# The attention tails of a fused attention and expert kernel on one core: one block tile for the tail keys of v, one tile for the tails of k and q, and another figure in the planner

## The chip, the core and the metric

The kernel runs on one core of one Trainium2 chip. The core's engines each run their own list of instructions in order: TensorE (PE, with its weight loads shown apart as PEld), VectorE (DVE), ScalarE (ACT), GpSimd (POOL), and SyncE (SP), which here only issues DMA transfers. Semaphores tie the lists together. The metric is the time of one execution in microseconds, the median of several; less is better. Before the change it is 1306.65 us, the median of three runs from 1305.46 to 1310.91 us.

## What is computed

There are 8 batches of 8 heads, 576 rows in each and 64 columns in a head, all in fp32. The first half is an attention that keeps the 32 largest scores of each row; the second sends each of the 4608 rows to one of 8 experts.

```python
scores = scale * np.matmul(q, k.transpose(0, 1, 3, 2))
kth = np.partition(scores, -top_k, axis=-1)[..., -top_k:-top_k + 1]
scores = np.where(scores >= kth, scores, -1e9)
attn = np.exp(scores - max) / (sum + 1e-9)
x = np.matmul(attn, v)                     # heads side by side: [4608, 512]
e_idx = np.argmax(x @ w_gate + modality_bias[modality_id], axis=1)
out = gate_w * (np.maximum(x @ w1[e], 0.0) @ w2[e])      # e = e_idx of the row
```

## The kernel before

**Pairs and tiles.** Two heads make a pair; there are 32 pairs. The 576 rows of a head are 4 blocks of 128 and a tail of 64. A pair is 9 tiles of 128 query rows: tiles 0 to 7 are the four blocks of the two heads in turn, and tile 8 holds the tail rows of both heads together. So there are 288 tiles, and the main loop (L865) makes one step for each, with a pipeline behind it: in step i the scores of tile i+2 are multiplied (`qk`, L324), the largest 32 values of tile i are looked for on VectorE (`subs`, `chain`, `find`, `pick`, L337 to L388), the masked weights of tile i-7 are formed there too (`keep`, L399), and tile i-9 is transposed on TensorE (`trans`, L414). VectorE's and GpSimd's parts are interleaved by hand.

**Weights by v.** `av` (L424) multiplies the transposed weights by v in five chunks of keys: four of 128 keys and a last one, c = 4, with the 64 tail keys. It runs three times for a pair: at tile 3 (query blocks 0 and 1), at tile 7 (blocks 2 and 3), both with 256 columns, and at tile 8 (the query tails, 64 columns). Each chunk is one matmul for each head; the two heads write the two halves of the output's partitions. The transposed tails of the two heads lie in the two halves of the partitions of `PT[:, :, 4]`, so in chunk 4 the tail of head 1 is read from partitions 64 to 127, for which `load` puts the tail of v of head 1 there a second time (L132). `av` hands its chunks out in pieces (AV3, AV7), one for a step.

**Tails of k and q.** `load` brings them as two tiles `kt` and `qt` of 64 partitions each. `prep(p, "t")` transposes both (L273), in step 0 of the pair before; the result goes through `split` to the operands of `qk`.

**The planner.** Expert work starts as soon as enough rows of finished batches are sorted. A list `moe` holds its pieces in order: transposes of the gathered rows `xg` (L690), the first layer (L702: `w1b`, `xgT`), the second layer (L714: `w2b`, `hT`). The loop keeps a credit `spare_pe`. Each step adds STEP = 3.3 us and takes off what the step's own TensorE work costs by the table COST (L53): 0.49 for one chunk of `av` with 256 columns. While the credit is over zero, pieces of `moe` are issued and their costs (0.22, 0.44 a matmul, 0.88) taken off (L960 to L971). An expert's slot of 256 rows is 8 such transposes, 32 products of the first layer and 16 of the second as they are written. 12 slots are started inside the loop; what is left of the list is issued after it (L1144). Then come the remaining slots with weights split in two parts (L1111, L1127).

Of the kernel before, what the change touches and what calls it, by code (L numbers as in the profile page):

```python
# [9 lines left out]
FT = mybir.dt.float32  # L10
# [39 lines left out]
PB = 4  # L50
AV3 = (0, 3, 5)
AV7 = (0, 2, 5)
COST = {"trans": 0.5, "qk": 0.5, "mix": 1.12, "rest": 0.22, "t": 0.11, "prep": 0.43, "logits": 1.2, "xrow": 0.54, "av": 0.49, "av8": 0.17}  # L53
RN = 6
QO = 0
FAST = 1
# [13 lines left out]
def kernel(  # L70
# [13 lines left out]
    V, A, G, PE, SP = nc.vector, nc.scalar, nc.gpsimd, nc.tensor, nc.sync  # L84
    B, H, S, D = q.shape
# [11 lines left out]
    const = ctx.enter_context(tc.tile_pool(name="const", bufs=1))  # L97
# [7 lines left out]
    ld = att.enter_context(tc.tile_pool(name="ld", bufs=2))  # L105
# [4 lines left out]


    LD, PR, T = {}, {}, {}
    PAUSE = lambda: None

    def load(p, what, b=None):

        o = LD.setdefault(p, {})
        h0 = 2 * (p % HP)
        for nm in what:
            src = {"k": k, "q": q, "v": v}[nm]  # L120
            g = src[p // HP] if b is None else src[ds(b, 1)].rearrange("o h s d -> (o h) s d")
            t = ld.tile([128 if nm == "v" else 64, 2, D], FT, name=nm + "t", bufs=2 if nm == "v" else 1)
            m = ld.tile([128, 2, 4, D] if nm == "v" else [128, 4, 2, D], FT, name=nm + "m", bufs=2 if nm == "v" else 1)
            if nm == "v":
                SP.dma_start(m.rearrange("p h c d -> p h (c d)"),
                             g[h0:h0 + 2, 0:512, :].rearrange("h (p c) d -> p h (c d)", c=4))
            else:
                for h in range(2):
                    SP.dma_start(m[:, :, h, :], g[h0 + h, 0:512, :].rearrange("(p c) d -> p c d", c=4))
            SP.dma_start(t[:64], g[h0:h0 + 2, 512:, :].rearrange("h p d -> p h d"))  # L130
            if nm == "v":
                SP.dma_start(t[64:, 1, :], g[h0 + 1, 512:, :])  # L132
            o[nm] = (m, t)

    load(0, "kq")
# [4 lines left out]
    idf = const.tile([128, 128], FT, name="idf")  # L140
# [26 lines left out]
    Pb = [wk.tile([128, 2 * S], FT, name=f"P{i}", bufs=1) for i in range(2)]  # L167
    Pm = const.tile([128, 640], FT, name="Pm")
    G.memset(Pm[:, S:], 0.0)
    xT = const.tile([128, HP + 2, S], FT, name="xT")  # L170
    xTs = lambda b: [xT[:, (b * HP + hp) % (HP + 2)] for hp in range(HP)]
    PT = const.tile([128, 4, 9, 128], FT, name="PT")
# [91 lines left out]
    def prep(p, part):  # L264


        d = PR.setdefault(p, {})
        if "st" not in d:
            d["st"] = wk.tile([128, 2, 2, S], FR, name="st", bufs=1)
        if part == "t":  # L270
            ps = psX.tile([128, 2, 64], FT, name="X")
            for x, nm in enumerate("kq"):
                PE.matmul(ps[:, x], LD[p][nm][1], idf[:64, :64], start=(x == 0), stop=False, is_transpose=True,  # L273
                          skip_group_check=True)
            split(*(d["st"][:, x, :, 512:] for x in range(2)), ps)
            return
        st = d["st"][:, :, "kq".index(part)]
        ps = psX.tile([128, 512], FT, name="X")
        for c in range(4):
            PE.matmul(ps[:, c * 128:(c + 1) * 128], LD[p][part][0][:, c], idf, start=(c == 0), stop=False,  # L280
                      is_transpose=True, skip_group_check=True)
        split(*(st[:, x, :512] for x in range(2)), ps)

        half = lambda x: slice(x * 64, x * 64 + 64)
        if part == "k":
            d["ks"] = wk.tile([128, 2, 2, S], FR, name="ks", bufs=2)
        else:
            d["qs"] = wk.tile([128, 2, S], FR, name="qs", bufs=2)

        def stack(h, queues=(SP, SP)):  # L290
            for v in range(2):
                if part == "k":
                    for a, b, o in ((0, S, 0),) if h == 0 else ((0, 512, 64), (512, S, -512)):
                        queues[v].dma_start(d["ks"][half(v), :, h, a + o:b + o].bitcast(FT), st[half(h), :, a:b].bitcast(FT))
                else:
                    queues[v].dma_start(d["qs"][half(v), h, :].bitcast(FT), st[half(h), v, :].bitcast(FT))

        for h in range(2):
            late_pe.append(lambda h=h, **o: stack(h, **o))
# [124 lines left out]
    def av(p, j, x):  # L424

        vm, vt = LD[p]["v"]
        w = 256 if j < 8 else 64
        st = {}

        def part(c0, c1):  # L430
            if c0 == 0:
                st["po"] = psX.tile([128, 256], FT, name="X")
            po = st["po"]
            for c in range(c0, c1):
                for h in range(2):
                    K = slice(0, 128) if c < 4 else slice(64, 128) if h and j < 8 else slice(0, 64)
                    l = vm[:, h, c, :] if c < 4 else vt[K, h, :]
                    if j < 8:
                        r = PT[K, j // 2 - 1:j // 2 + 1, c + 5 * h if c < 4 else 4, :]
                    else:  # L440
                        r = PT[K, 1, 4 + c, h * 64:h * 64 + 64]
                    o = po[h * 64:h * 64 + 64, :w]
                    PE.matmul(o.rearrange("p (a b) -> p a b", a=2) if j < 8 else o, l, r, start=(c == 0), stop=(c == 4))  # L443
            if c1 == 5:
                o = (j // 4) * 256
                xev.append(lambda: A.activation(x[:, o:o + w], po[:, :w], AF.Copy))
        cut = {3: AV3, 7: AV7, 8: (0, 5)}[j]
        return [((b - a) * COST["av" if j < 8 else "av8"], lambda a=a, b=b: part(a, b)) for a, b in zip(cut, cut[1:])]

# [415 lines left out]
    for i in range(LAST):  # L865
# [4 lines left out]

        cost = COST["trans"] * ok(i - TL)
        p, j = divmod(i, 9)
# [6 lines left out]
        if ok(i + QL):  # L879
            cost += COST["mix" if (i + QL) % 9 == 8 else "qk"]  # L880
        if QO == 0:
# [23 lines left out]
        for f in lp:  # L905
            f()
        cost += COST["rest"] * (len(lp) > 0)
        if p + 1 < NPAIR and j in PREP:
            prep(p + 1, PREP[j])
            cost += COST["t" if PREP[j] == "t" else "prep"]  # L910
        if p + 2 < NPAIR and j in LJ:
# [3 lines left out]
        b1, r = divmod(i - (TL + 2), 36)  # L915
        b1 -= 1
        if 0 <= b1 < B:
# [3 lines left out]
            if r == rl[0]:  # L921
                rows_of[b1] = logits(b1, xTs(b1))
                cost += COST["logits"]
            if r == rl[1]:
# [12 lines left out]
            if b1 == 0 and r == 8:  # L937
                head, tail = first_slot()
# [10 lines left out]
        if avs:  # L949
            c, f = avs.popleft()  # L950
            f()
            cost += c
        if ok(u) and u % 9 in (3, 7, 8):
            f = av(u // 9, u % 9, xTs(u // 36)[(u // 9) % HP])
# [6 lines left out]
        while seen[0] and spare_pe > 0:  # L961
# [4 lines left out]
            c, f, new = moe[0]  # L966
# [23 lines left out]
        for x in range(RN if rush else 0):  # L990
            f = rush.popleft() if rush else PAUSE
# [6 lines left out]
        for x in range(SN - len(small_)):  # L998
            f = side.popleft() if side and not rush else PAUSE
# [192 lines left out]
    ld = att.enter_context(tc.tile_pool(name="ldb", bufs=2))  # L1192
# [96 lines left out]
```

## Time and profile before

| | |
|---|---|
| median of 3 runs | 1306.65 us |
| profiled execution | 1310.04 us, its span 1308.2 us |
| TensorE busy | 1220.9 us, 93% of the span |
| VectorE busy | 1163.1 us, 89% |
| ScalarE, GpSimd busy | 1016.5 us, 685.9 us |
| last main tile formed on VectorE (L399) | starts at 1071.16 us |
| first matmul of the slots after the loop (L1111) | starts at 1122.55 us |

Times in the profile count from the start of the span. A matmul of fp32 operands appears as two records in the trace: the 768 products of v's 128-key chunks are 1536 records. A record's duration holds the way through the array, so neighbours overlap, and what one costs TensorE is read from the distance of the starts. The granted clock of TensorE is shown as a share of 2.4 GHz.

### The profile page before, as it was taken

What the parts mean: (1) busy time and instruction counts of PE and PEld (TensorE: products, weight loads), DVE (VectorE), ACT (ScalarE), POOL (GpSimd) and SP (SyncE); (2) the same over time, 40 slices, a digit from 0 to 9 for tenths busy, and PEclk for the clock granted to TensorE, in tenths of its full rate; (3) what the DMA queues carried; (4) which work ended last, traced back from release to release, by engine and by line L of the source; (5) the groups of instructions that cost most, each with busy time, mean ns of one, the idle gap of its engine ahead of it and who ended that gap; (6) DMA issues with size and microseconds to landing.
All of it is one profiled execution on the core that took longest, in us unless ns stands there. A gap on an engine that the chain in (4) does not pass through costs nothing. (4 is left out here: it accounts for less than half of the span.)

```text
span 1308.2 us, 29253 instructions
## 1 busy us (share of the span) xinstructions
PE 1220.9 (93%) x8149; PEld 926.4 (71%) x8149; DVE 1163.1 (89%) x5918; ACT 1016.5 (78%) x2037; POOL 685.9 (52%) x1330
## 2 busy tenths in 40 slices
PE   5888888899998999999999999999999998999986
PEld 4666666676775867677676767777676756789885
DVE  3999999999999999999999999999999973667752
ACT  3899988889887888898889889998888863445542
POOL 2555557546675557655856585658556753110110
PEclk7899999999999999999999999999999999999998
DMA  5565334676447746576656556666664534657550
GB/s 117 136 187 129 84 83 115 168 198 154 123 120 192 184 130 168 155 177 158 190 148 158 156 153 181 143 159 186 152 154 121 164 104 141 233 176 262 207 169 15
DMA packets 206791, 201.08 MB, mean 154 GB/s; under 512 B 106222, under 2 KB 153326, under 8 KB 206609
## 3 DMA queue, kind: packets, MB, share of 16 engines
q1 hardware_dynamic: 200400, 179.48, 52.0%
q0 software_dynamic: 6208, 19.54, 4.1%
q8 instruction: 70, 1.15, 0.4%
q14 instruction: 113, 0.92, 0.2%
HBM read 118.63 MB, written 24.23 MB: 109 GB/s over the span
## 5 line engine op out<-in xcount | busy, mean ns | idle before, releaser
L337 DVE MAX8 cand<-Ssb 128x8 f32<-128x82 f32 (+1 forms) x2016 | 433.4, 231 | 19.7 <-ACT Ssb L330 19.6
L375 POOL TENSOR_TENSOR y<-Ssb,K 128x576 f32<-128x576 f32 x288 | 368.1, 1278 | 9.8 <-ACT K L369 9.7
L324 PE MATMUL S<-ks,qs 128*128 128x288 f32 x1024 | 234.7, 352 | 48.6 <-ACT Ssb L330 27.8
L330 ACT ACTIVATE Ssb<-S 128x576 f32<-128x576 f32 x288 | 188.6, 655 | 91.3 <-PE S L324 77.0
L369 ACT ACTIVATE K<-Ssb,n 128x576 bf16<-128x576 f32 x288 | 227.3, 789 | 18.0 <-POOL y L375 17.7
L324 PEld LDWEIGHTS S<-ks,qs 128*128 128x128 f32 x1024 | 159.5, 193 | 105.5 <-ACT Ssb L330 42.7
L393 ACT ACTIVATE ex<-Ssb,sm 128x576 f32<-128x576 f32 x288 | 225.6, 783 | 0.0
L399 DVE SCALAR_TENSOR_TENSOR P<-Ssb,kth,ex 128x576 f32<-128x576 f32 x256 | 214.4, 838 | 2.6 <-PE T L414 1.4
L379 DVE MAX8 mg<-y 128x8 f32<-128x576 f32 x288 | 214.8, 746 | 2.0 <-POOL y L375 2.0
L422 ACT ACTIVATE PT<-T 128x640 f32<-128x640 f32 (+1 forms) x288 | 190.8, 663 | 10.0 <-PE T L414 10.0
L702 PE MATMUL E<-xgT,w1b 128*128 128x256 f32 x768 | 188.8, 389 | 4.1 <-ACT hT L706 2.7
L714 PE MATMUL E<-w2b,hT 128*128 128x512 f32 x384 | 185.6, 605 | 1.7 <-ACT ot L724 1.0
L414 PE MATMUL T<-idf,P 128*128 128x128 f32 x1152 | 170.8, 276 | 0.0
L443 PE MATMUL X<-PT,vm 128*64 128x256 f32 (+1 forms) x1536 | 160.7, 338 | 4.3 <-ACT st L261 2.5
L702 PEld LDWEIGHTS E<-xgT,w1b 128*128 128x128 f32 x768 | 139.9, 192 | 34.7 <-issue 5.8
L403 POOL TENSOR_SCALAR spare<-P 1x1 f32<-1x1 f32 x256 | 48.2, 188 | 209.6 <-DVE mg L348 193.6
L414 PEld LDWEIGHTS T<-idf,P 128*128 128x128 f32 x1152 | 136.8, 142 | 5.3 <-issue 2.7
L362 POOL TENSOR_SCALAR n<-mg 128x1 f32<-128x1 f32 x288 | 66.7, 232 | 114.2 <-DVE mg L350 102.9
L443 PEld LDWEIGHTS X<-PT,vm 128*64 128x64 f32 x1536 | 79.8, 136 | 56.4 <-issue 26.8
L714 PEld LDWEIGHTS E<-w2b,hT 128*128 128x128 f32 x384 | 66.0, 190 | 62.8 <-issue 54.2
L1133 POOL DMA_INDIRECT out_dram<-ot,tk x14 | 14.1, 1005 | 129.9 <-ACT ot L1132 129.9
L480 POOL TENSOR_TENSOR x<-x,rd 128x256 f32<-128x256 f32 (+1 forms) x80 | 52.7, 663 | 39.2 <-ACT x L484 36.2
(209 smaller groups left out, 2309.6 us busy)
## 6 DMA issues: line engine op xcount, KB each, us to landing
w1b<-in_moe_w_dram SPq DMA_DIRECT2D x76, 512.0 KB
w2b<-in_moe_w_dram SPq DMA_DIRECT2D x76, 512.0 KB
ks<-st SPq DMA_DIRECT2D x64, 288.0 KB
qs<-st SPq DMA_DIRECT2D x128, 144.0 KB
ks<-st SPq DMA_DIRECT2D x62, 256.0 KB
xg<-xs SPq DMA_DIRECT2D x19, 516.0 KB
km<-in_k_dram SPq DMA_DIRECT2D x64, 128.0 KB
qm<-in_q_dram SPq DMA_DIRECT2D x64, 128.0 KB
```

The costliest lines, as they stand in the source:

```text
L324: PE.matmul(ps[:, hf, u - a:v - a], l, d["ks"][:, x, h, u + o:v + o], start=(n == 0), stop=(n == len(terms) - 1), skip_group_check=(j == 8))
L337: return [lambda s=s: V.max(c[:, s * 8:s * 8 + 8], T[i]["S"][:, bnd[s]:bnd[s + 1]]) for s in range(NSUB)]
L369: A.activation(t["K"], t["S"], AF.Sign, scale=2.0 ** -24 - 1.0, bias=t["n"][:, 1, i % 3:i % 3 + 1], accum_out=t["n"][:, 0, i % 3:i % 3 + 1])
L375: G.tensor_tensor(t["y"], t["S"], t["K"], op=OP.mult)
L379: V.max(t["mg"][:, i % 3, 24:32], t["y"])
L393: A.activation(t["ex"], t["S"], AF.Exp, bias=t["s"][:, i % 3:i % 3 + 1])
L399: V.scalar_tensor_tensor(t["P"], t["S"], kth[:, i:i + 1], t["ex"], op0=OP.is_ge, op1=OP.mult, accum_out=dn)
L414: PE.transpose(T[i]["pt"][:, x, :], (Pm if c == 4 else Pb[c % 2])[:, h * 512 + x * 128:h * 512 + x * 128 + 128], idf)
L422: A.activation(o, T[i]["pt"][:, :n], AF.Copy)
L443: PE.matmul(o.rearrange("p (a b) -> p a b", a=2) if j < 8 else o, l, r, start=(c == 0), stop=(c == 4))
L702: PE.matmul(ps[:, f % 2], w1b[:, c, f * 128:(f + 1) * 128], xgT[:, c, :], start=(c == 0), stop=(c == KC - 1))
L714: PE.matmul(o["py"], hT[:, f, t * 128:(t + 1) * 128], w2b[:, f, :], start=(f == 0), stop=(f == FC - 1))
```

## The change

Three edits. (1) The tail tile of v becomes a fixed tile `vtb[p % 2]` of 128 partitions and three slots of 64 columns, zeroed once by VectorE. Head 0's tail goes to partitions 0 to 63 of slot 0, head 1's to partitions 64 to 127 of slot 1 and to partitions 0 to 63 of slot 2. Slots 0 and 1 together are a block-diagonal 128 by 128 operand, so chunk 4 with 256 columns is one matmul for both heads. For the query tails (tile 8) chunk 4 stays one matmul a head, now with all 128 partitions, of which the upper half is zero. (2) The tails of k and q are the two partition halves of one tile `kqt` and take one transpose. (3) COST["av"] is 0.46 instead of 0.49. Lines after the first edits lie some 7 to 11 lower in the changed file: L273, L324, L414, L443, L690, L702, L714, L1082 and L1111 of before are L280, L331, L421, L443 and L453, L701, L713, L725, L1093 and L1122 there.

```diff
-COST = {..., "av": 0.49, "av8": 0.17}
+COST = {..., "av": 0.46, "av8": 0.17}
...
+    vtb = [const.tile([128, 3, 64], FT, name=f"vt{i}") for i in range(2)]
...
+            if nm == "k":
+                o["kq"] = ld.tile([128, 2, D], FT, name="kqt", bufs=1)
+            t = vtb[p % 2] if nm == "v" else o["kq"][:64] if nm == "k" else o["kq"][64:]
...
-            SP.dma_start(t[:64], g[h0:h0 + 2, 512:, :].rearrange("h p d -> p h d"))
             if nm == "v":
+                tail = g[h0:h0 + 2, 512:, :].rearrange("h p d -> p h d")
+                SP.dma_start(t[:64, 0:3:2, :], tail)
                 SP.dma_start(t[64:, 1, :], g[h0 + 1, 512:, :])
+            else:
+                SP.dma_start(t, g[h0:h0 + 2, 512:, :].rearrange("h p d -> p h d"))
...
+    for t in vtb:
+        V.memset(t, 0.0)
...
-            for x, nm in enumerate("kq"):
-                PE.matmul(ps[:, x], LD[p][nm][1], idf[:64, :64], start=(x == 0), ...)
+            PE.matmul(ps.rearrange("p a b -> p (a b)"), LD[p]["kq"], idf, start=True, ...)
...
+                if c == 4 and j < 8:
+                    PE.matmul(po[:, :w]..., vt[:, 0:2, :].rearrange("p h d -> p (h d)"),
+                              PT[:, j // 2 - 1:j // 2 + 1, 4, :], start=False, stop=True, ...)
+                    continue
                 for h in range(2):
-                    K = slice(0, 128) if c < 4 else slice(64, 128) if h and j < 8 else slice(0, 64)
-                    l = vm[:, h, c, :] if c < 4 else vt[K, h, :]
+                    l = vm[:, h, c, :] if c < 4 else vt[:, 2 * h, :]
```

The edits move instructions on TensorE. The first place is one step of pair 29, with the transposes of its tile 0 of the pair before in the pipeline, the tails `kt` and `qt` (now `kqt`), and the two last pieces of `av` of a pair. Before:

```order
L414 MATMUL T<-idf,P_122 128x128 x4
L273 MATMUL X<-idf,kt 128x64
L273 MATMUL X<-idf,qt 128x64
L443 MATMUL X<-PT,vm 64x256 x4
L443 MATMUL X<-PT,vt 64x256 x2
L443 MATMUL X<-PT,vm 64x64 x8
L443 MATMUL X<-PT,vt 64x64 x2
```

The same place in the changed kernel:

```order
L421 MATMUL T<-idf,P_123 128x128 x4
L280 MATMUL X<-idf,kqt 128x128
L453 MATMUL X<-PT,vm 64x256 x4
L443 MATMUL X<-PT,vt_81 128x256
L453 MATMUL X<-PT,vm 64x64 x8
L453 MATMUL X<-PT,vt_81 64x64 x2
```

Two tail transposes are one, and the two `vt` products with 256 columns are one. Over the 32 pairs that is 64 products and 32 transposes less as they are written; no other count on TensorE changes.

The second place is the end of the main loop on TensorE: from the transposes of tile 283 to those of tile 287 (`Pm`, the last). Before:

```order
L414 MATMUL T<-idf,P_122 128x128 x4
L443 MATMUL X<-PT,vm 64x256 x6
L714 MATMUL E<-w2b,hT 128x512 x2
L414 MATMUL T<-idf,P_122 128x128 x5
L443 MATMUL X<-PT,vm 64x256 x2
L443 MATMUL X<-PT,vt 64x256 x2
L714 MATMUL E<-w2b,hT 128x512 x2
L414 MATMUL T<-idf,P_123 128x128 x4
L714 MATMUL E<-w2b,hT 128x512
L414 MATMUL T<-idf,P_123 128x128 x5
L690 MATMUL E<-idf,xg 128x128 x2
L414 MATMUL T<-idf,Pm 128x128 x5
```

In the changed kernel:

```order
L421 MATMUL T<-idf,P_123 128x128 x4
L453 MATMUL X<-PT,vm 64x256 x6
L701 MATMUL E<-idf,xg 128x128 x4
L421 MATMUL T<-idf,P_123 128x128 x5
L453 MATMUL X<-PT,vm 64x256 x2
L443 MATMUL X<-PT,vt_82 128x256
L713 MATMUL E<-xgT,w1b 128x256 x6
L421 MATMUL T<-idf,P_124 128x128 x4
L713 MATMUL E<-xgT,w1b 128x256 x2
L421 MATMUL T<-idf,P_124 128x128 x5
L713 MATMUL E<-xgT,w1b 128x256 x2
L421 MATMUL T<-idf,Pm 128x128 x5
```

The last of the twelve slots began with two of its `xg` transposes just ahead of tile 287; it now begins at tile 282 and has done 10 of its 32 first-layer products by tile 287.

The third place is after the loop on TensorE, from the last of the products that rank the rows of batch 7 (`ohb`) to the first product of the slots after the loop. Before:

```order
L535 MATMUL X<-ohb_148,onesb 128x8
L702 MATMUL E<-xgT,w1b 128x256 x16
L714 MATMUL E<-w2b,hT 128x512 x10
L1082 MATMUL X<-idf,xg 128x128 x8
L714 MATMUL E<-w2b,hT 128x512 x6
L1111 MATMUL X<-xgh,w1h 128x256
```

In the changed kernel:

```order
L546 MATMUL X<-ohb_151,onesb 128x8
L487 MATMUL X<-idf,xT 64x128 x4
L713 MATMUL E<-xgT,w1b 128x256 x12
L725 MATMUL E<-w2b,hT 128x512 x10
L1093 MATMUL X<-idf,xg 128x128 x8
L725 MATMUL E<-w2b,hT 128x512 x6
L1122 MATMUL X<-xgh,w1h 128x256
```

Behind the ranking stood 16 first-layer products and stand 12, with four of batch 7's row transposes (`xT`) that stood ahead of the ranking.

## Rows read from the trace of the kernel before

**Rows 1.** The page: busy time of the engines, then busy tenths in 40 slices.

```profile
PE 1220.9 (93%) x8149; PEld 926.4 (71%) x8149; DVE 1163.1 (89%) x5918; ACT 1016.5 (78%) x2037; POOL 685.9 (52%) x1330
...
PE   5888888899998999999999999999999998999986
...
DVE  3999999999999999999999999999999973667752
```

**Rows 2.** Stretches: length; PE, PEld, DVE, ACT, POOL busy us; clock; DMA share.

```profile
980.00:1040.00 60.00, 58.87 (x399) 41.64 (x399) 58.87 (x317) 52.76 (x111) 40.60 (x77) 1.00 0.49 136
1040.00:1057.00 17.00, 17.00 (x99) 12.36 (x96) 16.97 (x86) 13.54 (x27) 12.99 (x23) 1.00 0.57 181
1057.00:1079.50 22.50, 21.95 (x118) 11.20 (x116) 14.44 (x38) 12.63 (x23) 9.61 (x19) 1.00 0.27 85
1079.50:1122.50 43.00, 38.68 (x205) 25.19 (x206) 15.62 (x60) 14.05 (x25) 13.86 (x28) 1.00 0.42 137
```

**Rows 3.** Waits of DVE from 60 to 1060 us: us, times, longest.

```profile
DVE lt L511 <- PE X L503: 2.6, 5, 0.8
...
DVE P L399 <- PE T L414: 1.4, 2, 1.2
```

**Rows 4.** Timeline of DVE: start us, us, instruction, count, idle before and its end.

```profile
1071.16 0.82 DVE L399 SCALAR_TENSOR_TENSOR Pm<-Ssb,kth,ex 128x576 f32<-128x576 f32 x1 [0.73 <-ACT ex L393]
```

**Rows 5.** Timeline of PE around one transpose of the tails.

```profile
993.00 0.60 PE L414 MATMUL T<-idf,P 128*128 128x128 f32 x4
993.53 0.27 PE L273 MATMUL X<-idf,kt 64*128 64x64 f32 x1
993.64 0.23 PE L273 MATMUL X<-idf,qt 64*128 64x64 f32 x1
993.80 1.08 PE L443 MATMUL X<-PT,vm 128*64 128x256 f32 x8
994.81 0.65 PE L443 MATMUL X<-PT,vt 64*64 64x256 f32 x4
995.39 0.69 PE L443 MATMUL X<-PT,vm 128*64 128x64 f32 x16
996.01 0.33 PE L443 MATMUL X<-PT,vt 64*64 64x64 f32 x4
996.27 0.80 PE L324 MATMUL S<-ks,qs 128*128 128x288 f32 x4
```

**Rows 6.** Timeline of PE at the loop's end and behind it.

```profile
1048.74 2.76 PE L702 MATMUL E<-xgT,w1b 128*128 128x256 f32 x12
1051.34 0.71 PE L414 MATMUL T<-idf,P 128*128 128x128 f32 x5
...
1061.73 2.74 PE L714 MATMUL E<-w2b,hT 128*128 128x512 f32 x6
1064.31 0.60 PE L414 MATMUL T<-idf,P 128*128 128x128 f32 x4
1064.75 1.02 PE L714 MATMUL E<-w2b,hT 128*128 128x512 f32 x2
...
1079.50 0.77 PE L414 MATMUL T<-idf,Pm 128*128 128x128 f32 x5 [0.17 <-ACT PT L422]
...
1122.55 0.68 PE L1111 MATMUL X<-xgh,w1h 128*128 128x256 f32 x1
```

**Rows 7.** Timelines of DVE and POOL at one meeting of the two.

```profile
1041.43 1.26 DVE L387 TENSOR_TENSOR jk<-eq,mg 128x27 f32<-128x27 f32 x1
...
1041.38 1.27 POOL L375 TENSOR_TENSOR y<-Ssb,K 128x576 f32<-128x576 f32 x1
```

**Rows 8.** All instructions on tile eq: duration ns min/median/max, first and last start.

```profile
L386 DVE TENSOR_TENSOR eq<-i9s,n x96: 156/171/1200, 38.6 to 1068.1; 128x27 f32<-128x27 f32 x96
L387 DVE TENSOR_TENSOR jk<-eq,mg x96: 156/171/1267, 38.8 to 1068.3; 128x27 f32<-128x27 f32 x96
```

**Rows 9.** Two stretches behind the loop, columns as in rows 2.

```profile
1140.00:1160.00 20.00, 17.38 (x111) 16.00 (x110) 11.26 (x44) 7.43 (x13) 2.52 (x6) 0.91 0.55 184
...
1260.00:1280.00 20.00, 16.40 (x91) 14.83 (x90) 9.18 (x34) 6.03 (x11) 2.52 (x6) 0.83 0.09 30
```

More of the change, by code (lines that the diff above doesn't have):

```diff
@@ L52 @@
 AV7 = (0, 2, 5)
-COST = {"trans": 0.5, "qk": 0.5, "mix": 1.12, "rest": 0.22, "t": 0.11, "prep": 0.43, "logits": 1.2, "xrow": 0.54, "av": 0.49, "av8": 0.17}
+COST = {"trans": 0.5, "qk": 0.5, "mix": 1.12, "rest": 0.22, "t": 0.11, "prep": 0.43, "logits": 1.2, "xrow": 0.54, "av": 0.46, "av8": 0.17}
 RN = 6
@@ L121, in load @@
             g = src[p // HP] if b is None else src[ds(b, 1)].rearrange("o h s d -> (o h) s d")
-            t = ld.tile([128 if nm == "v" else 64, 2, D], FT, name=nm + "t", bufs=2 if nm == "v" else 1)
+            if nm == "k":
+                o["kq"] = ld.tile([128, 2, D], FT, name="kqt", bufs=1)
+            t = vtb[p % 2] if nm == "v" else o["kq"][:64] if nm == "k" else o["kq"][64:]
             m = ld.tile([128, 2, 4, D] if nm == "v" else [128, 4, 2, D], FT, name=nm + "m", bufs=2 if nm == "v" else 1)
@@ L271, in prep @@
             ps = psX.tile([128, 2, 64], FT, name="X")
-            for x, nm in enumerate("kq"):
-                PE.matmul(ps[:, x], LD[p][nm][1], idf[:64, :64], start=(x == 0), stop=False, is_transpose=True,
-                          skip_group_check=True)
+            PE.matmul(ps.rearrange("p a b -> p (a b)"), LD[p]["kq"], idf, start=True, stop=False, is_transpose=True,
+                      skip_group_check=True)
             split(*(d["st"][:, x, :, 512:] for x in range(2)), ps)
@@ L434, in part @@
             for c in range(c0, c1):
+                if c == 4 and j < 8:
+                    PE.matmul(po[:, :w].rearrange("p (a b) -> p a b", a=2), vt[:, 0:2, :].rearrange("p h d -> p (h d)"),
+                              PT[:, j // 2 - 1:j // 2 + 1, 4, :], start=False, stop=True, skip_group_check=True)
+                    continue
                 for h in range(2):
-                    K = slice(0, 128) if c < 4 else slice(64, 128) if h and j < 8 else slice(0, 64)
-                    l = vm[:, h, c, :] if c < 4 else vt[K, h, :]
+                    l = vm[:, h, c, :] if c < 4 else vt[:, 2 * h, :]
                     if j < 8:
-                        r = PT[K, j // 2 - 1:j // 2 + 1, c + 5 * h if c < 4 else 4, :]
+                        r = PT[:, j // 2 - 1:j // 2 + 1, c + 5 * h, :]
                     else:
-                        r = PT[K, 1, 4 + c, h * 64:h * 64 + 64]
+                        r = PT[:, 1, 4 + c, h * 64:h * 64 + 64]
                     o = po[h * 64:h * 64 + 64, :w]
-                    PE.matmul(o.rearrange("p (a b) -> p a b", a=2) if j < 8 else o, l, r, start=(c == 0), stop=(c == 4))
+                    PE.matmul(o.rearrange("p (a b) -> p a b", a=2) if j < 8 else o, l, r, start=(c == 0),
+                              stop=(c == 4), skip_group_check=True)
             if c1 == 5:
```

## The prediction

> **What bounds the kernel now.** I read the busy shares first. TensorE is busy 93% of the span and VectorE 89%, and the slices show where they part [rows 1]: VectorE is at 9 tenths or more from the second slice to the 32nd and falls off in the last eight, where TensorE stays at 8 to 9 until the very end. So there are two regimes. In the main loop VectorE has no idle time worth the name and TensorE is nearly full too. Behind the loop TensorE alone carries the time.
>
> The second view are the stretches around the loop's end [rows 2]. From 980 to 1040 us TensorE and VectorE are each busy 58.87 of 60 us. From 1040 to 1057 us TensorE is never idle, from 1057 to 1079.5 us it is busy 21.95 of 22.5, while VectorE drops to 14.44. VectorE starts its last tile at 1071.16 us [rows 4], TensorE transposes that tile only at 1079.50 us and reaches the slots behind the loop at 1122.55 us [rows 6]. From about 1040 us on the path is TensorE's list. Whatever shortens that list before its 1122.55 us comes off the end.
>
> The third view are VectorE's waits inside the loop. On TensorE's results it waits 2.6 us (logit rows) and 1.4 us (the buffer of weights that a transpose still reads) in 1000 us [rows 3]. That is all that a lighter TensorE can give back to VectorE directly.
>
> **The change part by part.** All prices are distances of starts.
>
> *Tails of k and q.* Before: from the four transposes at 993.00 us to the v products at 993.80 us, 0.80 us [rows 5]. Four transposes followed by work of the same full shape take 1064.75 - 1064.31 = 0.44 us, and followed by another shape 993.53 - 993.00 = 0.53 us [rows 5, 6], so a change of the array's shape costs 0.09 us. One transpose is a quarter of 0.44, 0.11 us. After: 0.44 + 0.11 + 0.09 = 0.64 us. Saved 0.16 us, 32 times: 5.1 us of TensorE (between 0 and 0.27 each, the whole of the two, 8.6 us).
>
> *The tail chunk with 256 columns.* Before: 994.81 to 995.39, 0.58 us for four records [rows 5]. After: two records of 128 by 128. The nearest row is the expert's first layer, same shape, type and columns: 12 records from 1048.74 to 1051.34 us, 0.217 each [rows 6], so 0.43 us. At tile 3 the neighbour behind it is full-shaped as well: saved 0.15. At tile 7 the query-tail products follow, a change of shape that I price at 0.09 again: saved 0.06. Together 32 x 0.21 = 6.7 us. The bounds: nothing saved (the new product costs the old 0.58), and 0.29 an instance (a pass as cheap as one of the old four, 0.145), 18.6 us.
>
> *The tail chunk of the query tails.* 996.01 to 996.27, 0.26 us, against 0.62 / 4 = 0.155 for a 128-key chunk of 64 columns ahead of it [rows 5], whose shape it now has. Saved 0.10, 32 times: 3.2 us (between 0, if the zero half costs something, and 0.26 - 0.11 = 0.15, 4.8 us).
>
> TensorE thus gets 5.1 + 6.7 + 3.2 = 15.0 us lighter over the program, 0.47 us a pair. In the Trainium skill, "TensorEngine Tiling (Array Packing)", section "Theoretical Speedup", a dimension of at most 64 is worth up to twofold through tiling, which would speak against a product at full size. By the trace four small records take 0.58 us where two full ones take 0.43, so no such gain is visible here. By that rule alone the second item would be zero and the sum 8.3 us; the same page's "Key Properties" says that a change of the tiling mode drains the engine, and the 0.09 us above agree.
>
> *The planner.* The figure 0.46 gives back 10 chunks x 0.03 = 0.30 us of credit a pair, which the planner fills with expert pieces. No slot starts earlier than its rows are there, so the lists of the two kernels are alike up to about tile 160 and drift apart only then. By the order of the instructions, from the transposes of tile 279 on the old kernel still has 29 second-layer products, 32 first-layer products and 8 transposes ahead of the slots behind the loop; the new one has 21, 32 and 8. Eight products of the second layer at 2 x 0.43 us (six records from 1061.73 to 1064.31 us [rows 6]) are 6.9 us. They are done in tiles 160 to 279 instead, 13 pairs, in which TensorE has 13 x 0.47 = 6.1 us less to do. So the loop carries them nearly for free, and the stretch in which TensorE sets the time is 6.9 us shorter. Of the 6.9 us, 5.0 lie behind the last tile's transposes (10 first-layer products at 0.43 and 6 transposes at 0.11 that are done ahead of them now) and 1.9 in the eight steps before. VectorE does not stand in the way: with 1.9 us less TensorE would transpose the last tile at 1077.6 us, well behind VectorE's 1071.16 + 0.82.
>
> *Waits and transfers.* The transfers are as many as before, of the same sizes. The first two tail loads of v wait for the zeroing; the two memsets stand ahead of VectorE's first work, for which it waits on ScalarE anyway, so I take zero (bounded by 1 us, as a tile of 576 columns takes 0.82 us [rows 4]). The products that now need both tail transfers of v, or of k and q, wait for the later one, as the pair of them did.
>
> *The sum.* 6.9 us of expert work out of the last stretch; 0.6 us from the tail chunks that lie in it (at 1040 to 1083 us: two with 0.15, two with 0.06, two with 0.10); and of the 4.0 us for which VectorE waits on TensorE [rows 3] a third, 1.3 us, as TensorE is lighter by a little but not empty. Together 8.8 us. The profiled execution took 1310.04 us, so it becomes 1301.2; it is 3.4 us above the median of 1306.65, and carried to that the time is 1298 us (0.7% less). The chances below speak of faster or slower by more than 0.5%, 6.5 us, about what a measurement can tell here: below 1300.1, above 1313.2.
>
> **The rivals.**
>
> *The loop pays for what the end saves.* TensorE is busy 58.87 of 60 us in the late loop [rows 2]. If the full-size product costs the old 0.58 us, and the change of shape is dearer than 0.09, TensorE is freed of 0.2 us a pair while 0.3 us is booked on it. Also, work put into steps in which TensorE is already late delays ScalarE, and that the loop. Of the 6.9 us some 4 come back as a longer loop, and the gain is 3 to 5 us: 1302 to 1304. For it: both engines are at 98%. Against it: the measured distances, and that VectorE's waits on TensorE are 4.0 us in 1000.
>
> *TensorE sets the loop as well.* Then all 15.0 us count, since the expert work is the same in sum: 1306.65 - 15 = 1292. For it: late in the loop TensorE has hardly any idle time. Against it: VectorE has none either.
>
> *VectorE and GpSimd collide more often.* At 1041.43 us a VectorE product of 27 columns took 1.26 us while GpSimd's product ran from 1041.38 us for 1.27 [rows 7]; its median is 0.17 us and the worst 1.27 [rows 8]. It ended when GpSimd's did. Expert pieces that move by up to five steps move ScalarE's evacuations, hence the moment at which GpSimd starts. In the 13 pairs that change there are 3 x 2 such small products and 9 masked tiles a pair, 195 chances; a collision costs up to 1.1 us. It turns the forecast of -8.8 into slower by 6.5 from 14 or 15 more collisions on. 20 more give 1306.65 - 8.8 + 22 = 1320. For it: nothing in the code ties GpSimd's start to these small products. Against it: as many may vanish as appear.
>
> *The planner's figure does nothing.* If the pieces were held back by their data rather than by the credit, the lists would be alike at the end and only 0.6 + 1.3 us would be gained, 1305; the order speaks against it.
>
> Beside these, the clock: behind the loop the granted share falls to 0.91 and 0.83 in two stretches [rows 9], which means 1.2 GHz for a part of each, in the first behind some us without a product. A shift of the whole end by 9 us may win or lose one such fall, 2 to 3 us either way; I keep it in the range.
>
> **How the numbers follow.** The forecast (1294 to 1302) gets 0.50, the loop that pays 0.28, TensorE as the bound of all 0.10, more collisions 0.07, no shift 0.05. Faster by over 0.5%: four fifths of the forecast (0.40), all of the third (0.10), a little of the first rival (0.04), 0.54. Slower: 0.06, most of the collisions' case. The rest, 0.40, is within 0.5%. The range of 8 in 10 is 1291 to 1307: it leaves out part of TensorE's case below and the collisions above.
>
> **What would show it.** Right: the last tile is still formed near 1071 us; TensorE transposes it near 1077 instead of 1079.5, and the first L1111 product (now L1122) starts near 1114. The tail chunk shows two records of 128 by 128, 0.22 us apart, and the step with the tails' transpose is 0.16 us shorter. The stretch from there to the end stays 185.7 us long (1122.55 to 1308.2). Wrong in the first rival's way: the last tile on VectorE comes 3 to 5 us later. Wrong in the third's: the mean of the small products on VectorE rises well over its present level and the loop ends later still. Wrong altogether: the stretch behind the loop changes its own length, through the clock or a transfer.

## The result and the profile after

| kernel | median us (runs) | ratio to before, 95% interval |
|---|---|---|
| before | 1308.78 (4) | |
| changed | 1295.92 (4, from 1291.75 to 1298.71) | 0.989 [0.9867, 0.9914] |
| changed, once more in a later group of runs | 1294.12 (4) | 0.9877 [0.9856, 0.9897] |

The forecast was 1298, with faster by over 0.5% the likeliest. The time fell by 12.9 us where 8.8 were expected, and it fell by another way than the forecast's, as the experiments show. The profiled execution after took 1297.98 us, its span is 1296.1 us.

First the pieces on TensorE, in the step of pair 29 that [rows 5] show for before (timeline: start, time from first to last, line, records):

```profile
991.31 0.60 PE L421 MATMUL T<-idf,P 128*128 128x128 f32 x4
991.74 0.27 PE L280 MATMUL X<-idf,kqt 128*128 128x128 f32 x1
991.95 1.08 PE L453 MATMUL X<-PT,vm 128*64 128x256 f32 x8
992.96 0.70 PE L443 MATMUL X<-PT,vt 128*128 128x256 f32 x2
993.59 0.69 PE L453 MATMUL X<-PT,vm 128*64 128x64 f32 x16
994.11 0.29 PE L453 MATMUL X<-PT,vt 128*64 128x64 f32 x4
994.32 0.80 PE L331 MATMUL S<-ks,qs 128*128 128x288 f32 x4
```

From the transposes to the v products it is 0.64 us, 0.16 less, as priced. The tail chunk takes 0.63 us (992.96 to 993.59), not the 0.52 that I had booked with its change of shape, and more than the 0.58 of before. The query tails behind it gain on both parts: 0.52 and 0.21 where it was 0.62 and 0.26. So tiles 7 and 8 together save 0.10 us and not 0.16. At tile 3 the next fence has the chunk: 1069.35 to 1069.88, 0.53 us against 0.58. There the other 0.10 us comes from the neighbour, which now follows a product of its own shape: behind a narrow one, six second-layer records took 2.68 us (1052.43 to 1055.11), behind a full one 2.57 (1059.53 to 1062.10). The whole is 0.16 + 0.10 + 0.15 = 0.41 us a pair, 13.1 us where 15.0 were booked.

Second, the end of TensorE's list after, against [rows 6], and VectorE's last tile, against [rows 4]:

```profile
1052.43 2.84 PE L725 MATMUL E<-w2b,hT 128*128 128x512 f32 x6
1055.11 0.60 PE L421 MATMUL T<-idf,P 128*128 128x128 f32 x4
...
1059.53 2.74 PE L725 MATMUL E<-w2b,hT 128*128 128x512 f32 x6
1062.10 0.60 PE L421 MATMUL T<-idf,P 128*128 128x128 f32 x4
...
1069.35 0.70 PE L443 MATMUL X<-PT,vt 128*128 128x256 f32 x2
1069.88 2.75 PE L713 MATMUL E<-xgT,w1b 128*128 128x256 f32 x12
...
1075.59 0.71 PE L421 MATMUL T<-idf,Pm 128*128 128x128 f32 x5
...
1111.51 0.68 PE L1122 MATMUL X<-xgh,w1h 128*128 128x256 f32 x1
...
1069.66 0.81 DVE L406 SCALAR_TENSOR_TENSOR Pm<-Ssb,kth,ex 128x576 f32<-128x576 f32 x1
```

The last tile is transposed 3.9 us earlier (1077 was expected), the slots behind the loop start 11.0 us earlier (1122.55 before, 1114 expected). VectorE too forms its last tile 1.5 us earlier (1071.16 before), where the forecast had it unmoved: the loop itself has become shorter.

Third, four stretches of the whole run, cut in each kernel at the same five events: VectorE's first work on the masked tiles 9, 72 and 279, the first product of the slots behind the loop, the end. Columns as in [rows 2]. Before:

```profile
71.91:290.43 218.52, 190.05 (x1515) 145.75 (x1512) 217.18 (x1205) 191.74 (x389) 126.20 (x246) 0.99 0.52 133
290.43:1053.47 763.04, 747.63 (x4932) 549.66 (x4930) 750.96 (x4025) 663.52 (x1374) 487.81 (x922) 1.00 0.61 158
1053.47:1122.55 69.08, 64.22 (x339) 38.10 (x337) 33.61 (x116) 29.59 (x54) 25.08 (x49) 1.00 0.37 120
1122.55:1308.25 185.70, 167.50 (x1059) 152.36 (x1057) 110.88 (x283) 87.25 (x135) 18.71 (x44) 0.95 0.53 180
```

After:

```profile
71.71:290.57 218.86, 192.28 (x1481) 148.78 (x1478) 217.22 (x1204) 191.35 (x389) 126.29 (x246) 0.98 0.52 132
290.57:1051.34 760.77, 743.45 (x4832) 555.96 (x4830) 750.87 (x4025) 664.97 (x1375) 489.63 (x924) 0.99 0.61 159
1051.34:1111.51 60.17, 56.24 (x316) 35.17 (x315) 32.90 (x116) 28.88 (x53) 26.53 (x47) 1.00 0.40 130
1111.51:1296.13 184.62, 166.44 (x1059) 151.29 (x1057) 110.70 (x283) 87.28 (x135) 18.71 (x44) 0.96 0.53 181
```

The first stretch (pairs 1 to 7) is unchanged. The late loop (pairs 8 to 30) is 2.3 us shorter, the stretch behind it 8.9, the slots behind the loop 1.1. I call these four the early loop, the late loop, the exit and the rest.

### The profile page after: what moved, and what is told of

It is laid out like the page before. It is cut to its first block, busy times and chain, and to the rows that moved or that the text cites. A ratio compares the mean times of both kernels' runs of the same rounds, so it can differ in the third digit from the quotient of the medians.

```text
span 1296.1 us, 29003 instructions
## 1 busy us (share of the span) xinstructions
PE 1207.1 (93%) x7989; PEld 929.3 (72%) x7989; DVE 1162.5 (90%) x5920; ACT 1016.7 (78%) x2037; POOL 689.3 (53%) x1330
## 5 line engine op out<-in xcount | busy, mean ns | idle before, releaser
L331 PE MATMUL S<-ks,qs 128*128 128x288 f32 x1024 | 234.6, 351 | 50.6 <-ACT Ssb L337 29.3
L376 ACT ACTIVATE K<-Ssb,n 128x576 bf16<-128x576 f32 x288 | 226.9, 788 | 12.8 <-POOL y L382 12.3
L331 PEld LDWEIGHTS S<-ks,qs 128*128 128x128 f32 x1024 | 158.8, 192 | 106.7 <-ACT Ssb L337 43.5
L713 PE MATMUL E<-xgT,w1b 128*128 128x256 f32 x768 | 187.6, 387 | 2.8 <-ACT hT L717 1.5
L725 PE MATMUL E<-w2b,hT 128*128 128x512 f32 x384 | 183.9, 601 | 1.7 <-ACT ot L735 1.0
L421 PE MATMUL T<-idf,P 128*128 128x128 f32 x1152 | 171.2, 276 | 0.6 <-ACT PT L429 0.6
L453 PE MATMUL X<-PT,vm 128*64 128x256 f32 (+1 forms) x1536 | 162.7, 340 | 4.3 <-ACT st L269 2.5
L713 PEld LDWEIGHTS E<-xgT,w1b 128*128 128x128 f32 x768 | 141.0, 192 | 29.3 <-ACT hT L717 3.9
L421 PEld LDWEIGHTS T<-idf,P 128*128 128x128 f32 x1152 | 136.7, 142 | 4.7 <-ACT PT L429 1.7
L453 PEld LDWEIGHTS X<-PT,vm 128*64 128x64 f32 x1536 | 80.4, 137 | 58.3 <-issue 31.3
L725 PEld LDWEIGHTS E<-w2b,hT 128*128 128x128 f32 x384 | 66.9, 190 | 58.6 <-issue 50.8
```

Of the source, the lines that this page charges most:

```text
L331: PE.matmul(ps[:, hf, u - a:v - a], l, d["ks"][:, x, h, u + o:v + o], start=(n == 0), stop=(n == len(terms) - 1), skip_group_check=(j == 8))
L376: A.activation(t["K"], t["S"], AF.Sign, scale=2.0 ** -24 - 1.0, bias=t["n"][:, 1, i % 3:i % 3 + 1], accum_out=t["n"][:, 0, i % 3:i % 3 + 1])
L421: PE.transpose(T[i]["pt"][:, x, :], (Pm if c == 4 else Pb[c % 2])[:, h * 512 + x * 128:h * 512 + x * 128 + 128], idf)
L713: PE.matmul(ps[:, f % 2], w1b[:, c, f * 128:(f + 1) * 128], xgT[:, c, :], start=(c == 0), stop=(c == KC - 1))
L725: PE.matmul(o["py"], hT[:, f, t * 128:(t + 1) * 128], w2b[:, f, :], start=(f == 0), stop=(f == FC - 1))
```

## The experiments

Theory A is the forecast's: VectorE paces the loop, TensorE only the exit, and the gain is expert work that leaves the exit. Rival B is the forecast's second rival: TensorE paces the loop as well, so that all its work counts.

### The planner's figure alone

```diff
-... "av": 0.49, ...        # the kernel before
+... "av": 0.46, ...
```

> The kernel before with COST['av'] 0.46 and nothing else. Its TensorE list carries the same expert pieces per step as the changed kernel (21 second-layer products left from the transposes of tile 279 on, 29 before) but none of the cheaper tails. Theory A (VectorE paces the loop, TensorE the end; the gain is the 6.9 us of expert work that leaves the end): 5 to 8 us faster than before, L1111 starts 6 to 8 us earlier, the last main tile on VectorE moves by less than 2 us. Rival B (TensorE paces the loop as well, so only its total work counts, which is unchanged here): within 2 us of before, the loop ends some 6 us later and the end gives it back.

Measured: 1307.56 us against 1308.59, ratio 0.9986 [0.9967, 1.0004]. Late loop and exit:

```profile
290.05:1061.78 771.73, 753.50 (x4947) 554.21 (x4948) 755.37 (x4025) 664.12 (x1373) 489.93 (x924) 0.99 0.59 157
1061.78:1122.81 61.03, 57.11 (x325) 35.38 (x326) 32.97 (x116) 29.36 (x54) 26.05 (x47) 1.00 0.40 128
```

The exit is 8.1 us shorter (69.08 before), nearly as much as after the whole change. The late loop is 8.7 us longer (763.04): TensorE is busy 5.9 us more, against 6.9 us for the eight pieces that moved, and idle 2.8 us more. The granted clock plays a small part: it is at half (0.50) for 13.6 us of this late loop and for 6.8 us of that before, and TensorE is busy for 9.7 and 5.8 us of these, so that by an estimate, half the busy time, 2 us of the 8.7 are the clock's. Even so the loop is 6.7 us longer, where A has less than 2. The work moved, and the time shows next to nothing won. A is refuted, B holds: pieces put into the late loop are paid for there.

### The tiles alone

```diff
-... "av": 0.46, ...        # the changed kernel
+... "av": 0.49, ...
```

> The changed kernel with COST['av'] back at 0.49: the cheaper tails without the credit; 29 second-layer products are left from tile 279 on, as before. Theory A: 1 to 4 us faster than before (0.4 to 0.6 us of tail chunks in the last stretch, 1 to 3 us less waiting in the loop), L1111 1 to 4 us earlier. Rival B: the 13 us that TensorE is freed of all count, 11 to 14 us faster. If A holds for this and the run with the credit alone, the two add to the whole change; if the whole is more than the sum, the credit needs the room that the tiles make.

Measured: 1299.91 us, ratio 0.9932 [0.9917, 0.9946], 8.9 us by the ratio:

```profile
290.25:1045.59 755.34, 738.63 (x4822) 552.33 (x4822) 747.86 (x4024) 664.66 (x1375) 487.59 (x922) 1.00 0.61 160
1045.59:1113.83 68.24, 63.38 (x329) 38.01 (x325) 33.61 (x116) 28.89 (x53) 25.03 (x49) 1.00 0.37 122
```

The late loop is 7.7 us shorter, the exit 0.8. TensorE is freed of 23 x 0.41 = 9.4 us there. It lies between the numbers of the two theories, and the split shows why: only the pairs from 8 on pay. The two parts, 1.4 per mille and 6.8, are less than the whole's 11.0 to 12.3. By the ratios the rest is 3.7 to 5.4 us, with intervals nearly as wide; by the profiled stretches it is 3.3 us, for with the tiles the credit costs the late loop 5.4 us and without them 8.7, while the exit gains 8.1 both times. That the credit uses room which the tiles made is the likely reason, and not shown by itself.

### A padding on TensorE and one on VectorE

Both add 0.44 us a pair to the changed kernel, one on each engine. The second ran beside the changed kernel as its control:

> The changed kernel once more, as the control beside the other three on this chip. Both theories: ratio to before within its first interval, 0.987 to 0.991.

```diff
-            PE.matmul(ps..., LD[p]["kq"], idf, ...)
+            for _ in range(5):
+                PE.matmul(ps..., LD[p]["kq"], idf, ...)
```

> The changed kernel with the transpose of the tails of k and q done five times instead of once (the same result): 4 x 0.109 = 0.44 us more on TensorE in each pair, 14 us over the program, 13.5 of it inside the loop, with no new wait and the same planner. Theory A (VectorE paces the loop): 0 to 4 us slower than the changed kernel. Rival B (TensorE paces it): 12 to 14 us slower.

```diff
-        return [lambda s=s: V.max(...) for s in range(NSUB)]
+        return [lambda s=s: V.max(...) for s in [0] * (3 if i % 9 == 5 else 0) + list(range(NSUB))]
```

> The changed kernel with the first of the seven MAX8 of a tile done four times in one tile of each pair: three more instructions of 0.146 us, 0.44 us a pair on VectorE, 14 us over the program, the size of the padding that TensorE had. Theory A (VectorE paces the loop): 10 to 14 us slower than the control. Theory B (TensorE paces it from pair 8 on): 3.5 us from the first 8 pairs and at most 5 from the rest, 3 to 8 us slower. If both paddings cost nearly their full size, the two engines are in step and neither is the bound alone.

Measured: TensorE padded 1306.21 us, ratio 0.9987 [0.9971, 1.0002], so 13 to 14 us slower than the changed kernel by its two ratios, 10 to 12 by its two medians. VectorE padded 1298.57 us, ratio 0.9913 [0.9894, 0.9933], 4.4 us by the medians over its control in the same group (1294.12). Its profiled execution is the fastest of its six, 1294.77 us, as fast as the control's 1294.75. Early and late loop of the control:

```profile
70.43:289.87 219.44, 188.50 (x1481) 145.96 (x1478) 217.69 (x1205) 191.74 (x389) 125.60 (x246) 1.00 0.51 131
289.87:1049.90 760.03, 743.79 (x4833) 555.86 (x4830) 750.58 (x4024) 664.64 (x1374) 490.78 (x924) 0.99 0.61 160
```

With TensorE padded:

```profile
71.93:290.71 218.78, 191.42 (x1504) 149.76 (x1501) 217.69 (x1205) 191.15 (x388) 125.51 (x246) 0.99 0.52 132
290.71:1059.14 768.43, 753.49 (x4925) 566.60 (x4923) 753.41 (x4024) 664.81 (x1374) 487.81 (x924) 0.99 0.60 158
```

With VectorE padded:

```profile
72.20:294.68 222.48, 191.22 (x1482) 148.09 (x1479) 220.78 (x1225) 191.76 (x389) 126.00 (x246) 0.98 0.51 128
294.68:1051.64 756.96, 742.80 (x4834) 555.32 (x4834) 751.04 (x4093) 664.88 (x1375) 486.29 (x924) 1.00 0.61 160
```

In the stretches the two are nearly mirror images. In the early loop TensorE's padding costs nothing (218.78 against 219.44) and VectorE's costs its size (222.48, +3.0 for 7 x 0.44). In the late loop TensorE's costs 8.4 us for 10, and VectorE's costs nothing here (756.96, even 3 less). As the profiled execution is a fast one, the medians are the safer measure: of their 4.4 us the early loop takes 3.0, so 1.4 us are left for all that follows. VectorE did 69 instructions more there (4093 records against 4024), 10 us at 0.146 each, and was busy 751.04 us against 750.58. So in this execution its 98.8% were not full: the added work fitted in while other instructions became shorter. Part of that is seen in the two small products that meet GpSimd's work. By line, with busy us and mean ns, in the control's late loop:

```profile
L393 DVE TENSOR_TENSOR eq<-i9s,n 128x27 f32<-128x27 f32 x69 | 20.4, 296 | 0.0
...
L394 DVE TENSOR_TENSOR jk<-eq,mg 128x27 f32<-128x27 f32 x69 | 19.6, 285 | 0.1
```

and with VectorE padded:

```profile
L393 DVE TENSOR_TENSOR eq<-i9s,n 128x27 f32<-128x27 f32 x69 | 18.1, 262 | 0.0
L394 DVE TENSOR_TENSOR jk<-eq,mg 128x27 f32<-128x27 f32 x69 | 17.8, 258 | 0.1
```

Together they are 4.1 us shorter, 35.9 us; in the late loops of the other 13 profiles they take 37.4 to 42.4 us, so part of the 4.1 is chance from run to run. VectorE paces pairs 1 to 7, TensorE the rest.

### The parts of the tiles

The kernel before with one part of the change each, both with 0.49:

```diff
-            for x, nm in enumerate("kq"):                     # tails of k and q alone
-                PE.matmul(ps[:, x], LD[p][nm][1], idf[:64, :64], ...)
+            PE.matmul(ps..., LD[p]["kq"], idf, ...)
```

> The kernel before with the tails of k and q in one tile and one transpose, nothing else (COST['av'] 0.49, the tail of v as before). Theory B (from pair 8 on TensorE paces the loop, so 24 of 32 pairs count): 24 x 0.16 = 3.8 us faster than before. Theory A: within 1.5 us of before.

```diff
+                if c == 4 and j < 8:                          # tail of v alone
+                    PE.matmul(po..., vt[:, 0:2, :]..., PT[:, j // 2 - 1:j // 2 + 1, 4, :], ...)
+                    continue
```

> The kernel before with the tail of v in the block tile, nothing else (COST['av'] 0.49, k and q as before). Theory B: 0.15 us a pair at tile 3 and 0.10 at tiles 7 and 8 together, 24 pairs, 6 us, 5 to 7 us faster than before; with the transposes' 3.8 that makes what the tiles alone gave. Theory A: 0.5 to 2 us faster.

Measured: 1303.92 us, 0.9962 [0.9944, 0.998], 5.0 us; and 1303.1 us, 0.9963 [0.994, 0.9985], 4.8 us. In the profiles the late loop is 5.2 and 3.4 us shorter than before. The sum of the two gains, 9.8 us, stands against the tiles' 8.9. The intervals reach down to 2.6 and 2.0 us, so both gains lie at or above the top of A's numbers (1.5 and 2). They are too wide to tell B's 3.8 and 6 us apart.

### A narrow chunk at tile 7

```diff
-                if c == 4 and j < 8:        # the changed kernel
+                if c == 4 and j == 3:
...
-                    l = vm[:, h, c, :] if c < 4 else vt[:, 2 * h, :]
+                    l = vm[:, h, c, :] if c < 4 else vt[:, h, :] if j == 7 else vt[:, 2 * h, :]
...
-                        r = PT[:, j // 2 - 1:j // 2 + 1, c + 5 * h, :]
+                        r = PT[:, j // 2 - 1:j // 2 + 1, c + 5 * h if c < 4 else 4, :]
```

> The changed kernel, but chunk 4 at tile 7 is one product of 128 by 64 for each head out of the zero-padded tile, as the four chunks ahead of it; at tile 3 it stays block-diagonal. In the trace after, the chunk at tile 7 takes 0.63 us (1056.66 to 1057.29) as it changes the array's shape on both sides; without the change it should take about 0.51, and the products of 64 columns behind it should no longer start late. Saved some 0.1 to 0.15 us a pair, 3 to 5 us of TensorE. Theory A: 0 to 1.5 us faster than the changed kernel. Rival B: 3 to 5 us faster.

> Chunk 4 at tile 7 narrow, as in the run of that name, beside the control. Theory B (TensorE paces the loop from pair 8 on): the products of a pair's end take 0.1 to 0.15 us less on TensorE, 24 pairs count, 2.5 to 3.5 us faster than the control. Theory A (VectorE paces the loop): within 1 us of the control.

Measured: 1291.48 us, 0.9876 [0.9854, 0.9897]; again, beside the control of 1294.12 us: 1287.74 us, 0.9839 [0.9818, 0.9859]. The second is 6.4 us faster than the changed kernel by the medians, 5.0 by the ratios. The first, in a group of runs without the changed kernel, shows 0 to 2 us by the ratios and 2.6 to 4.4 by the medians. The place in this kernel (second run), then its late loop:

```profile
1046.17 1.08 PE L453 MATMUL X<-PT,vm 128*64 128x256 f32 x8
1047.09 0.60 PE L453 MATMUL X<-PT,vt 128*64 128x256 f32 x4
1047.52 0.63 PE L453 MATMUL X<-PT,vm 128*64 128x64 f32 x16
1047.98 0.29 PE L453 MATMUL X<-PT,vt 128*64 128x64 f32 x4
1048.20 1.12 PE L725 MATMUL E<-w2b,hT 128*128 128x512 f32 x2
```

```profile
289.62:1042.20 752.58, 735.74 (x4885) 558.40 (x4885) 745.73 (x4025) 664.28 (x1375) 489.69 (x924) 0.99 0.61 161
```

From the first v product to the next work: 1048.20 - 1046.17 = 2.03 us, where the changed kernel needs 994.32 - 991.95 = 2.37. I had expected 0.1 to 0.15 us less and it is 0.34, because without the change of shape the neighbours on either side are quicker too: the eight records ahead take 0.92 instead of 1.01, the chunk 0.43 instead of 0.63, the sixteen behind 0.46 instead of 0.52. Over 23 pairs that is 7.8 us, and the late loop is 7.5 us shorter than the control's. The granted clock is at half for 10.2 us in both. B holds, with a price from the wrong place.

### More credit, and fewer pieces

On the narrow chunk, first the figure 0.43, then the tile 3 chunks in one piece, then that with 0.42:

```diff
-... "av": 0.46, ...
+... "av": 0.43, ...
```

> The narrow chunk at tile 7 and COST['av'] 0.43. Three second-layer products more leave the end (18 instead of 21 are left from tile 279 on), 2.6 us. Theory B: the loop pays about as much as the end saves, within 1.5 us of the run with the narrow chunk. Theory A: 2 to 3 us faster than that.

```diff
-AV3 = (0, 3, 5)
+AV3 = (0, 5)
```

> The kernel with the narrow chunk at tile 7, and AV3 = (0, 5): the five chunks at tile 3 are issued in one piece instead of two, so TensorE goes into the narrow shape and out of it once less a pair, about 0.3 us (0.09 in; out of it 0.31 instead of 0.21 and a first product that is 0.1 late). The planner then leaves 29 second-layer products for the end, as in the kernel before. Theory B: 24 x 0.3 = 7 us of TensorE less, but without the credit's use of idle time, 3 to 7 us faster than the run with the narrow chunk. Theory A: the end is 9 us longer again and the loop no shorter, 6 to 9 us slower than that run.

> The kernel with the narrow chunk at tile 7 and the chunks of tile 3 in one piece, with COST['av'] 0.42: from tile 279 on 16 + 10 fewer pieces are left (31.0 us of work ahead of the slots behind the loop instead of 43.1 with 0.46). Theory B: TensorE is idle 21.6 us in the loop of the run with one piece, more than in any other; the 12 us put there are paid for in part, the stretch from tile 279 to L1111 becomes 54 to 56 us (66.3), the loop from tile 72 to 279 750 to 757 us (746.0): 0 to 5 us faster than that run, ratio to before 0.983 to 0.987. Against it: with 0.43 the kernel with two pieces lost 4 us; if the pieces again meet steps that are full, no gain or 1 to 4 us slower.

Measured: 1292.9 us, 0.9867 [0.9847, 0.9887]; 1292.15 us, 0.9868 [0.9847, 0.9889]; 1300.29 us, 0.9918 [0.9896, 0.994]. All three expectations missed. With 0.43 the kernel is 5.2 us slower than with 0.46 by the medians. In the profiles both stretches are longer, the late loop 757.35 us (752.58) and the exit 61.18 (59.15), though this profile is of the slowest of its four executions, 1296.66 us. Of the 4.8 us in the late loop 4.1 are TensorE's idle time, most of it in waits for the transfer of the next pair's q (12.3 us against 8.6). Against the two medians of the narrow chunk with two pieces the second run is 0.7 and 4.4 us slower, the third 8.8 and 12.6. Late loop and exit of the two:

```profile
291.00:1037.03 746.03, 724.42 (x4872) 555.50 (x4872) 741.88 (x4025) 664.66 (x1375) 485.62 (x922) 1.00 0.62 162
1037.03:1103.32 66.29, 61.95 (x330) 37.89 (x327) 33.35 (x116) 29.04 (x53) 25.02 (x49) 1.00 0.39 125
```

```profile
290.91:1059.59 768.68, 742.91 (x4897) 564.62 (x4895) 754.22 (x4028) 664.79 (x1374) 492.48 (x926) 0.99 0.60 160
1059.59:1113.34 53.75, 48.86 (x303) 32.53 (x304) 27.21 (x88) 28.49 (x54) 24.60 (x46) 1.00 0.35 116
```

With one piece the late loop is 6.6 us shorter (746.03 against 752.58) and the exit 7.1 us longer (66.29 against 59.15): the planner, by the same figure 0.46, leaves eight second-layer products more to the end (64 of their records in the exit, against 48), 6.9 us of work. I had seen that and still counted a gain of 3 to 7 us on top. It did not come. TensorE is busy 11.3 us less in the late loop, so beside the work that left some 4 us were freed (some 2 of them, by the same estimate, are the granted clock's: TensorE is busy at half for 3.4 us against 7.1), but it is idle 4.8 us more: it waits longer for ScalarE, to clear the score buffer (`Ssb`, 6.4 us against 2.6) and to hand over the first layer's result (`hT`, 4.4 against 1.1).

With 0.42 the exit falls by 12.5 us and the late loop grows by 22.7. There the late loop holds TensorE idle for 768.68 - 742.91 = 25.8 us, and the two longest of its waits, in the run with one piece and in this one (waits of TensorE in the late loop: us, times, longest), are

```profile
PE S L331 <- ACT Ssb L337: 6.4, 10, 1.2
PE S L331 <- DMA qs<-st: 5.9, 3, 4.5
```

```profile
PE S L331 <- DMA qs<-st: 12.9, 5, 6.5
PE S L331 <- ACT Ssb L337: 5.6, 8, 1.2
```

The wait for the next pair's q is 7.0 us longer, TensorE's idle time in sum 4.2 us. The other 18.5 of the 22.7 us are busy time. Sixteen second-layer products and four transposes more in the loop make 14.2 us of it at the prices above. The granted clock makes some 6 us more by the estimate: TensorE is busy at half for 15.9 us of this late loop, against 3.4 in the run with one piece. Together that is a little more than the 18.5. All four falls come in or just behind such a wait. One of the four places (the wait in brackets, then the stretch behind it with its clock, the third number from the end):

```profile
921.68 0.76 PE L331 MATMUL S<-ks,qs 128*128 128x288 f32 x4 [1.69 <-DMA qs<-st]
922.40:925.80 3.40, 3.40 (x12) 2.87 (x11) 3.37 (x26) 3.40 (x8) 1.89 (x4) 0.50 0.78 175
```

So by this estimate such a wait can cost TensorE more than its own length.

At the exit's end the slots behind the loop now have to wait 2.33 us (idle time in brackets); the profile names no releaser, but ScalarE forms their operands `w1h` and `xgh` only from 1110.77 us and 1112.66 us on:

```profile
1109.98 1.04 PE L1093 MATMUL X<-idf,xg 128*128 128x128 f32 x8
1113.34 0.39 PE L1122 MATMUL X<-xgh,w1h 128*128 128x256 f32 x1 [2.33 <-issue]
```

The best version found is the one with the narrow chunk at tile 7 and 0.46: 1291.48 and 1287.74 us.

## Why the prediction was right and where it was wrong

**Right.** The direction and the time within its range, the second in part by luck, as will be seen. The exit: 6.9 + 0.6 us were booked, 8.9 measured, and the run with the credit alone gives 8.1 of it to the credit. TensorE is idle 0.9 us less there (69.08 - 64.22 = 4.9 us, 3.9 after); the remaining 0.5 us are open. The transposes of k and q: 0.16 us as priced; the run that has them alone gained 5.0 us, and its interval, 2.6 to 7.3, holds the 3.8 expected for 24 pairs. The transfers and memsets: no cost is seen, the early loop starts at 71.71 us (71.91 before) and is as long.

**Wrong: what bounds the loop.** "That is all that a lighter TensorE can give back to VectorE directly" is the step that failed, and with it the 1.3 us in the sum. I read VectorE's 98 to 99% busy and its 4.0 us of waits on TensorE as proof that VectorE paces the loop. The paddings show that from pair 8 on TensorE does: 10 us more on VectorE cost the late loop nothing in its profile and 1.4 us at most by the medians, 10 us more on TensorE cost 8.4. The rows had a hint that I passed over. In the early loop TensorE leaves 28 us of the 218.5 idle, and 44 us of what it does there are the 318 filler products of `keep_warm` (L842), which the loop issues until the first rows are sorted; expert work starts only at 253.9 us. In the late loop it was idle 15.4 of 763.04 us before, and it is idle for 15 to 18 us after, with the credit alone, with the tiles alone and with the padding. The idle time of an engine that only follows would change with its load. TensorE's does not in these five, and the length does. In the three runs that missed their expectations (0.43, and the two with one piece) it rose to 21 to 26 us: there waits on ScalarE and on q's transfer came in, so not every piece taken off or put on TensorE shows in full.

**Wrong by the same step: "the loop carries them nearly for free".** The credit alone lengthens the late loop by 8.7 us, more than the exit saves. In the whole change the late loop paid 5.4 us for the credit (760.77 against 755.34) out of the 7.7 that the tiles gave it (by the estimate the granted clock makes 1.7 of the 5.4, TensorE being busy at half for 7.1 us against 3.7). The forecast had put the first at nearly nothing and the second at 1.3, and the two errors, 5.4 and 6.4 us, nearly cancel: that is the luck in a forecast whose time fits. The gain that shows in the exit was earned in the loop: the planner carried it there. That is the second rival ("all 15.0 us count", 1292), less what the early loop swallows (8 pairs of 32) and with the smaller price: 23 x 0.41 = 9.4 us plus 0.8 in the exit, 10.2. I gave it a chance of 0.10. In the profiled executions the slots behind the loop start 11.0 us earlier, and the rest takes 1.1 us less at a granted share of 0.96 instead of 0.95; the control's has 0.97 and 182.86 us, so this last part comes and goes with the clock. The medians differ by 12.9 us; what the median has beyond these I cannot assign.

**Mis-sized: the full-size chunk.** 0.43 us was taken from the expert's first layer in mid-stream. Behind a narrow product the second of the two records starts 0.32 us after the first instead of 0.217, so the chunk is 0.53, and 0.63 where a narrow product follows. At tile 3 that cancels against the neighbour, which is spared the same lateness; at tile 7 the change loses 0.05 us on the chunk. The 0.09 us for a change of shape was only its first half: the narrow chunk at tile 7, which does the same work without the change there and back, is worth 0.34 us each time. The Trainium skill ("TensorEngine Tiling (Array Packing)", section "Key Properties") says that a change of the tiling mode drains the engine. The trace agrees with it in these 0.34 us.

**The other rivals.** Collisions between VectorE and GpSimd did not become more: the two small products together took 40.5 us in the late loop after and 42.3 before. The planner's figure does move work, as the order said.

## What to carry to other kernels

Two engines at 98% each do not tell which one paces. VectorE's waits on TensorE were 4.0 us in 1000, and yet the late loop's length followed TensorE's load; VectorE was busy 98.8%, and yet 10 us more fitted in. Add the same small padding to each engine in turn and see in which stretch the time follows. And a planner's figure moves work, it does not remove any: what it seems to win at the end has to be looked for in the loop that took the work. And look at the granted clock of each stretch before its length is explained: by the estimate used here it cost these late loops between 2 and 8 us.

## What the runs showed of the hardware that I had not expected

A change between products of 128 by 128 and 128 by 64 costs more than the 0.09 us between two starts: behind the change the work starts late too (2.68 against 2.57 us for six records), and the way out costs as well (eight narrow records take 1.01 us to the start of a full one and 0.92 to the start of a narrow one), so that a chunk of two records between narrow neighbours costs 0.34 us more than the same work done as four narrow records. And VectorE, with 69 instructions added, was in one profiled execution busy 0.5 us longer and not 10. Its small products `eq` and `jk` were 4.1 us shorter there, and five more of its groups (on `s_av`, `Pm`, `r_pb`, `sei` and `base`) 6.2 us, time that had been counted as busy; why all of them came out shorter in that execution is open. Last, in the late loops of all 14 profiles the granted clock fell to half only in, or within 1.4 us behind, a wait of TensorE for the transfer of the next pair's q, of 1.7 to 8.0 us, and stayed there for 3.4 to 10.2 us. Not every such wait was followed by a fall: one of 3.0 us with the figure 0.43 (up to 783.80 us) was not.
